# Reordering the head of a recurrent attention and feed-forward kernel: later zeroing, fewer idle products, one early gate/value piece, earlier states

## The chip, the cores and the metric

The kernel runs on one core of one Trainium2 chip. The metric is the device time of one execution in microseconds. Before the change the median of three runs is 625.0 us (624.94 to 625.14). The profiled execution took 625.15 us, and its trace spans 623.3 us. Every time inside the kernel is counted from the start of that span.

## The reference

Two blocks follow each other. The first is a recurrence over time for 4 batches, 8 heads, 768 steps and head size 48:

```python
for t in range(S):
    cur = einsum('bhd,bhe->bhde', u[None] * k_t, v_t)
    y[:, :, t] = einsum('bhd,bhde->bhe', r_t, state + cur)
    state = w[None, :, :, None] * state + einsum('bhd,bhe->bhde', k_t, v_t)
```

The second is a feed-forward block on the result, reshaped to 3072 tokens of 384 numbers: `(silu(x @ w_gate) * (x @ w_val)) @ w_out`, with 1536 inner columns. Everything is float32.

## The kernel before

The kernel cuts time into chunks of 128 steps. One chunk of one batch is a unit, so there are 24 units, and units 0 to 3 are the first chunks of the four batches. Inside a unit the recurrence becomes products of matrices: k and r are transposed and scaled by powers of the decay w (turn), their product gives a score matrix (scores) that is copied under a mask into At, whose diagonal holds the term of u (own_product, own_sum, diagonal). At times v gives the unit's outputs (outputs), and k times v adds to the batch's state Z (update). Unit 4 is the second chunk of batch 0 and so the first that reads a state.

The order in which the Python code emits the instructions is the order in which each engine runs them. There is no scheduler behind it. Engines wait for each other by semaphores.

The parts used below (cuts marked with ...):

```python
dve, pool, act, pe, sp = nc.vector, nc.gpsimd, nc.scalar, nc.tensor, nc.sync
ps_a = ... (name="ps_a", bufs=4, PSUM)      # scores, transposes, outputs, states
...
def own_product(i):                          # GpSimd, two instructions
    pool.tensor_mul(rk, rl, kl)
    pool.tensor_mul(rk, rk, ub[:])
def own_sum(i):                              # VectorE
    dve.tensor_reduce(dus[i][:], rks.pop(i), axis=AX.X, op=ALU.add)
def scale_k(i):
    pool.tensor_mul(khat[i % 4][:, :, 0:D], raw(i)[0], kscale[:])
def diagonal(i):                             # four heads on ScalarE, four on GpSimd
    small.extend(lambda h=h: act.activation(At[i % 2][:, h, :], ident[:], AF.Identity, scale=du[:, h : h + 1]) ...)
    pool.tensor_mul(At[i % 2][:, on_act:H], ident ..., du ...)
def turn(i):
    for tp, t, dst, table in zip(...):
        for a in range(HP):
            pe.transpose(tp[:, a, :], pair(t, a), ident[:])
        if i < 4:
            dve.tensor_mul(dst[:], tp[:], table)
        else:
            act.copy(dst[:], tp[:])
def scores(i):
    ...                                      # eight products into two PSUM tiles
    for e in range(2):
        dve.copy_predicated(At[i % 2] ..., mask ..., ps[e][:])
def outputs(i):
    ...                                      # products At x v, and from unit 4 on Z x rT
    act.copy(xT[:, i % NX, :, :], ps[:])
def update(i):
    ...                                      # products k x v into u_ps
    for e in range(2):
        if c == 0:
            dve.tensor_mul(ze, ps[rows], w)  # w is w128
        else:
            dve.tensor_add(ze, ps[rows], ze)
            pool.tensor_mul(ze, ze, w)
def gate_value(g, f):                        # a "piece": six products
    ...
    act.activation(sg[:], gv[:, 0, :], AF.Sigmoid)
    dve.tensor_mul(sg[:], sg[:], gv[:, 0, :])
    dve.tensor_mul(hT[g][:, f, :], sg[:], gv[:, 1, :])
```

The weights of the second block come in 18 chunks. Each is rounded on three engines before TensorE uses it: ScalarE makes a scaled high part (round_high) and a low part (round_low), VectorE puts the bits in place (round_dve), and GpSimd adds the low part (add_low for half a chunk, round_pool for a whole one). The low part has two buffers, so round_low of a chunk waits until GpSimd has added the low part of the chunk two before it.

`warm(n)` issues n products of the identity with itself whose results nobody reads. They keep TensorE busy while it would otherwise wait. `feed(1)` emits the next piece, once its weights are rounded.

The head of the program, in the order of emission:

```python
for z in Z:
    pool.memset(z[:], 0.0)
... # loads of w, of k and r of units 0 and 1, u, first weights, v
make_identity(nc, ident[:])                  # GpSimd
warm(18)
pool.memset(mask[:], 1.0) ...
... # decay tables on VectorE, pw and pv
own_product(0)
turn(0); natural_tables(); own_sum(0); diagonal(0)
own_product(1); load(2); load_weights(); load_v(2); warm(3)
turn(1); load(3); load_v(3); scores(0)
own_sum(1); diagonal(1)
... # first half of weight chunk 0
scores(1); warm(2); scale_k(0); add_low(0, 0); outputs(0)
... # first half of weight chunk 1
own_product(2); scale_k(1); outputs(1); queue(0)
for n in range(2):
    round_high(n, 1, n); round_dve(n, 1); add_low(n, 1)
load_weights()
turn(2); feed(1); own_sum(2); diagonal(2)
own_product(3); turn(3)
dve.tensor_copy(w128[:].unsqueeze(2), pw[:, :, 0:1])
scores(2); update(0); update(1)
own_sum(3); diagonal(3); scores(3)
scale_k(2); outputs(2); load(4)
round_act(); feed(1)
outputs(3); scale_k(3)
round_act(); round_pool(); scale(4); load_v(4); feed(1)
update(2); update(3)
round_pool(); own_product(4); load(5); feed(1)
...
```

From here a loop over the units follows, with pieces of the feed-forward block fed between their parts.

Of the kernel before, what the change touches and what calls it, by code (L numbers as in the profile page):

```python
# [22 lines left out]
def fast(  # L23
# [44 lines left out]
    dve, pool, act, pe, sp = nc.vector, nc.gpsimd, nc.scalar, nc.tensor, nc.sync  # L68
# [6 lines left out]
    w128 = cst.tile([P, HP], FP32, name="w128")  # L75
# [11 lines left out]
    Z = [cst.tile([P, HP, D2], FP32, name=f"Z{b}") for b in range(B)]  # L87
# [14 lines left out]
    def rhat_of(i):  # L102
        return rhat[i % 2 if i < BLOCKS else i % 4 // 2]

    def raw(i):

        if i < 4:
            return khat[i][:, :, 0:D], rhat[i % 2][:, :, 0:D]
        return k_ld[i % 2][:], r_ld[i % 2][:]
# [32 lines left out]
    def next_chunk(stage):  # L142
        n = done[stage]
        done[stage] = min(n + 1, NW)
        return n if n < NW else None

    def load_weights():
        n = next_chunk("load")
        if n is not None:
            src = chunks[n][0].bitcast(INT32)  # L150
            bits[n] = three.tile([P, WN, 2], INT32, name="w_bits", tag="w_bits")
            sp.dma_start(
                out=bits[n][:].rearrange("p (c f) two -> p c (f two)", c=src.shape[1]), in_=src
            )
# [13 lines left out]
    def round_high(n, half, bank):  # L168
        hi = halves(bits[n][:, :, 1], n)[half]
        ps, tag = ((ps_w, "w_mag"), (ps_o, "o"))[bank]  # L170
        mag = ps.tile([P, WN // 2], INT32, name="w_mag", tag=tag)
        mags[n, half] = mag[:].rearrange("p (c f) -> p c f", c=hi.shape[1])
        act.activation(
            mags[n, half].bitcast(FP32), hi.bitcast(FP32), AF.Copy, scale=float(2.0**-112)
        )

    def round_low(n):
        lows[n] = two.tile([P, WN], INT32, name="w_low", tag="w_low")
        act.activation(
            lows[n][:], bits[n][:, :, 0].bitcast(UINT32), AF.Copy, scale=float(2.0**-29)  # L180
        )

    def round_dve(n, half):
        hi = mags.pop((n, half))
        f = hi.shape[2]
        dst = chunks[n][1].bitcast(INT32)
        dst = dst[:, :, half * f : half * f + f] if hi.shape[1] == 3 else dst[:, half : half + 1]
        dve.tensor_scalar(dst, hi, -(1 << 31), None, ALU.bitwise_and)
        dve.scalar_tensor_tensor(dst, hi, 3, dst, ALU.logical_shift_left, ALU.bitwise_or)

    def add_low(n, half):

        dst = chunks[n][1].bitcast(INT32)
        f = dst.shape[2] // 2
        cols = slice(half * f, half * f + f)
        low = lows[n][:].rearrange("p (c f) -> p c f", c=dst.shape[1])
        pool.tensor_tensor(dst[:, :, cols], dst[:, :, cols], low[:, :, cols], ALU.add)

    def round_act(next_load=1):
        n = next_chunk("act")  # L200
        if n is not None:
            round_high(n, 0, 0)
            round_low(n)
            round_dve(n, 0)
            round_high(n, 1, 1)
            round_dve(n, 1)
            del bits[n]
            for _ in range(next_load):
                load_weights()
# [15 lines left out]
    def own_product(i):  # L225
        kl, rl = raw(i)
        rk = two.tile([P, H, D], FP32, name="rk", tag="rk")[:]
        pool.tensor_mul(rk, rl, kl)  # L228
        pool.tensor_mul(rk, rk, ub[:])
        rks[i] = rk  # L230

    def own_sum(i):
        dus[i] = three.tile([P, H], FP32, name="du", tag="du")
        dve.tensor_reduce(dus[i][:], rks.pop(i), axis=AX.X, op=ALU.add)
# [4 lines left out]
        dve.memset(t[:, :, D:64], 0.0)  # L239
    dve.memset(hats[:, 0:6, :, D:64], 0.0)  # L240
    dve.memset(wcol[:], 1.0)
    for z in Z:
        pool.memset(z[:], 0.0)
    for e in range(2):
        sp.dma_start(out=wcol[64 * e : 64 * e + D, :], in_=w.rearrange("(a e) d -> e d a", e=2)[e])
    load(0)
# [12 lines left out]
    def warm(n):  # L259

        ps = ps_a.tile([P, HP, P], FP32, name="warm", tag="a")
        for _ in range(n):
            pe.matmul(ps[:, 0, :], ident[:], ident[:], start=True, stop=True)

    warm(18)

    pool.memset(mask[:], 1.0)
    pool.affine_select(
        out=mask[:], in_=mask[:], compare_op=ALU.is_gt, fill=0.0,
        base=0, pattern=[[1, P]], channel_multiplier=-1,  # L270
    )
    dve.tensor_scalar(held[:], wcol[:], W_LOW, W_HIGH, ALU.max, ALU.min)
    tables = two.tile([P, 2, HP, P + 32], FP32, name="tables", tag="hT")
    pw, pv = tables[:, 0, :, 0 : P + 1], tables[:, 1, :, 0:P]
    dve.memset(pw[:, :, P : P + 1], 1.0)
    dve.tensor_copy(pw[:, :, P - 1 : P], held[:].unsqueeze(2))
    for l in range(7):
        n = 1 << l
# [19 lines left out]
    def scale_k(i):  # L298
        pool.tensor_mul(khat[i % 4][:, :, 0:D], raw(i)[0], kscale[:])  # L299
# [4 lines left out]
    def natural_tables():  # L304
        for t, dst in ((pw[:, :, 1 : P + 1], kscale), (pv, rscale)):
            t_ps = ps_a.tile([P, HP, P], FP32, name="t_ps", tag="a")
            for a in range(HP):
                pe.transpose(t_ps[:, a, :], t[:, a, :], ident[:])
            act.copy(dst[:], t_ps[:].rearrange("p a (e x) -> p (a e) x", e=2)[:, :, 0:D])
# [5 lines left out]
    def diagonal(i):  # L315

        du = dus.pop(i)
        on_act = HP if i < 4 else H
        small.extend(
            lambda h=h: act.activation(  # L320
                At[i % 2][:, h, :], ident[:], AF.Identity, scale=du[:, h : h + 1]
            )
            for h in range(on_act)
        )
        if on_act < H:
            n = H - on_act
            pool.tensor_mul(
                At[i % 2][:, on_act:H], ident[:].unsqueeze(1).to_broadcast([P, n, P]),
                du[:, on_act:H].unsqueeze(2).to_broadcast([P, n, P]),
            )  # L330

    def pair(t, a):
        return t[:, 2 * a : 2 * a + 2, :].rearrange("p e d -> p (e d)")

    def turn(i):
        kr = khat[i % 4], rhat_of(i)
        tps = [ps_a.tile([P, HP, P], FP32, name="tp", tag="a") for _ in kr]
        turned[i] = three.tile([P, HP, P], FP32, name="rT", tag="rT")
        for tp, t, dst, table in zip(tps, kr, (kT[i % 2], turned[i]), (pw[:, :, 1 : P + 1], pv)):
# [6 lines that stand above are left out]
# [69 lines left out]
    def update(i):  # L415
        c, b = divmod(i, B)
        if c == NCH - 1:
            return
        kh, vl, z = khat[i % 4], v_ld[i % 4], Z[b]
        ps = ps_a.tile([P, HP, D], FP32, name="u_ps", tag="a")  # L420
        for a in range(HP):
            for q in range(4):
                e, half = divmod(q, 2)
                pe.matmul(  # L424
                    ps[32 * q : 32 * q + 32, a, :], kh[:, 2 * a + e, 32 * half : 32 * half + 32],
                    vl[:, a, 64 * e : 64 * e + D],
                    start=True, stop=True, skip_group_check=True,
                )
        for e in range(2):
            rows = slice(64 * e, 64 * e + D)  # L430
            ze = z[rows, :, D * e : D * e + D]
            w = w128[rows].unsqueeze(2).to_broadcast([D, HP, D])
            if c == 0:
                dve.tensor_mul(ze, ps[rows], w)
# [3 lines that stand above are left out]
# [238 lines left out]
    def feed(n, pops=1):  # L676
        for _ in range(n):
            ready = [k for k, (need, _) in enumerate(todo) if need <= done["pool"] + len(summed)]
            if ready:
                todo.pop(ready[0])[1]()  # L680
            for _ in range(min(pops, len(small))):
                small.popleft()()
# [40 lines left out]
    def flush():  # L723
        while small:
            small.popleft()()
# [2 lines left out]
    turn(0)  # L728
    natural_tables()
    own_sum(0)  # L730
    diagonal(0)
    flush()
    own_product(1)
# [20 lines left out]
    round_low(1)  # L754
    round_dve(1, 0)
    add_low(1, 0)
    own_product(2)
    scale_k(1)
    outputs(1)
    queue(0)  # L760
    for n in range(2):
        round_high(n, 1, n)
        round_dve(n, 1)
        add_low(n, 1)
        del bits[n], lows[n]
    done.update(act=2, pool=2)
    load_weights()
    turn(2)
    feed(1)
    own_sum(2)  # L770
    diagonal(2)
    flush()
    own_product(3)
    turn(3)
    dve.tensor_copy(w128[:].unsqueeze(2), pw[:, :, 0:1])
    scores(2)
    update(0)
    update(1)
# [8 lines left out]
    feed(1)  # L787
    outputs(3)
    scale_k(3)
    round_act()  # L790
    round_pool()
    scale(4)
    load_v(4)
    feed(1)
    update(2)
    update(3)
    round_pool()
    own_product(4)
    load(5)
# [464 lines left out]
```

## Time and profile before

| what | value |
|---|---|
| time, median of three runs | 625.0 us |
| span of the trace | 623.3 us |
| TensorE busy | 611.0 us |
| TensorE busy from 600 us to the end (23.3 us) | 17.98 us |
| GpSimd busy from 41.0 to 54.7 us (13.7 us) | 13.46 us |
| VectorE busy from 20.7 to 30.0 us (9.3 us) | 9.04 us |
| zeroing of the four states, GpSimd | 0.80 to 2.28 us |
| first product of TensorE | 2.84 us |
| transposes of unit 3, second half | 25.34 us |
| outputs of unit 4, first product | 57.76 us |

PE is TensorE, PEld its weight loads, DVE VectorE, ACT ScalarE, POOL GpSimd, SP SyncE, which only issues transfers here. In the list of waits a line names who waited, for whom, the total in us, how often, and the longest. In the chain of waits a line has start, length, and what filled that time; the chain is followed back from the last instruction to whatever released it. In a timeline a line has start, length, engine, source line, operation, output and inputs, and shapes. L341 is turn, L379 and L384 are scores, L409 is outputs, L424 and L434 are update, L448 to L456 are a gate/value piece, L228 and L229 are own_product, L234 is own_sum, L299 is scale_k, L173, L179, L188, L189, L197 and L216 are the rounding of weights.

### The profile page before, as it was taken

The page shows a single profiled execution, that of the slowest core. Times are in us where ns is not written, and L with a number is a line of the kernel's source. Part 1 is how long each engine was busy: PE and PEld are TensorE (multiplying, and loading weights), DVE is VectorE, ACT ScalarE, POOL GpSimd, SP SyncE. Part 2 cuts the span into 40 slices and gives each one's busy share as a digit, 9 for nine tenths or more (in the row PEclk, how much of TensorE's full clock was granted, in tenths as well). Part 3 has the DMA queues.
Part 4 walks back from the last instruction along what each step waited for, and adds up shares of the span by engine and source line. Part 5 has one row for each costly group of instructions (what it writes and reads, how often), then busy time and mean ns, then how long its engine had stood idle before and what let it go on. Part 6 is the DMA issues. An engine that isn't in the chain of part 4 may idle for free.

```text
span 623.3 us, 13014 instructions
## 1 busy us (share of the span) xinstructions
PE 611.0 (98%) x5040; PEld 552.1 (89%) x5040; DVE 358.6 (58%) x751; ACT 238.9 (38%) x647; POOL 296.9 (48%) x350
## 2 busy tenths in 40 slices
PE   8799999999999999999999999999999999999996
PEld 7688888899888899888899888899988899988896
DVE  6888997373566574466575355574354463355460
ACT  3368785312444412344331335422243321233310
POOL 4789789935556315364452636341334211443110
PEclk9999999999999999999999999999999999999999
DMA  7989873233232213322223312221000000000001
GB/s 187 218 215 252 260 242 65 50 62 82 57 60 34 40 16 76 65 42 46 44 34 70 78 16 32 31 41 38 26 1 2 2 0 26 26 1 2 1 2 56
DMA packets 138008, 40.47 MB, mean 65 GB/s; under 512 B 128592, under 2 KB 131792, under 8 KB 137936
## 3 DMA queue, kind: packets, MB, share of 16 engines
q1 hardware_dynamic: 134480, 34.82, 26.4%
q10 hardware_dynamic: 3456, 4.72, 2.1%
q8 instruction: 42, 0.69, 0.5%
q14 instruction: 30, 0.25, 0.1%
HBM read 28.51 MB, written 4.72 MB: 53 GB/s over the span
## 4 chain that ended last, share of the span: by engine, by line
PE 90%; POOL 2%; DMA 1%; ACT 1%; DVE 1%; issue 0%; SPq 0%; ACTq 0%; POOLq 0%
PE c_b L625 25%; PE c_a L625 21%; PE o_f L519 13%; PE o_a L519 8%; PE gv L448 7%; PE o_b L519 6%; PE y_ps L409 5%; PE s_ps L379 3%; PE u_ps L424 1%; PE tp L341 1%; DMA r_ld<-in_r_dram 1%; POOL wg L216 1%; POOL wv L216 1%; POOL rk L228 0%; POOL hats L299 0%
## 5 line engine op out<-in xcount | busy, mean ns | idle before, releaser
L609 POOL TENSOR_TENSOR hT<-hT,u 128x256 f32<-128x256 f32 x60 | 47.0, 785 | 148.7 <-DVE hT L608 121.6
L632 ACT COPY u<-c_a 128x256 f32<-128x256 f32 x120 | 44.5, 371 | 85.8 <-PE c_a L625 83.3
L625 PE MATMUL c_a<-t,wv 128*128 128x256 f32 x240 | 72.1, 382 | 0.1
L625 PE MATMUL c_b<-xT,wg 128*128 128x256 f32 x240 | 71.7, 380 | 0.0
L605 ACT ACTIVATE sg<-hT 128x256 f32<-128x256 f32 x120 | 50.0, 416 | 52.5 <-DVE hT L634 33.8
L320 ACT ACTIVATE At<-ident,du 128x128 f32<-128x128 f32 x176 | 62.0, 398 | 16.0 <-DVE o_sb L533 7.2
L625 PE MATMUL c_b<-xT,s 128*128 128x256 f32 x240 | 61.7, 380 | 0.0
L639 DVE TENSOR_TENSOR u<-u,c_b 128x256 f32<-128x256 f32 x60 | 25.1, 419 | 60.5 <-PE c_b L625 55.4
L625 PEld LDWEIGHTS c_a<-t,wv 128*128 128x128 f32 x240 | 45.0, 190 | 6.8 <-ACT u L632 1.2
L625 PEld LDWEIGHTS c_b<-xT,s 128*128 128x128 f32 x240 | 45.3, 190 | 6.5
L625 PEld LDWEIGHTS c_b<-xT,wg 128*128 128x128 f32 x240 | 45.4, 190 | 5.9
L634 DVE TENSOR_TENSOR hT<-p,c_b 128x256 f32<-128x256 f32 x60 | 25.2, 420 | 41.7 <-PE c_b L625 39.1
L585 POOL TENSOR_TENSOR s<-wv,wg 128x256 f32<-128x256 f32 x24 | 17.6, 734 | 65.5 <-PE o_f L519 50.8
L384 DVE COPY_PREDICATED At<-mask,s_ps 128x512 f32<-128x512 int32 x48 | 33.0, 741 | 21.3 <-PE s_ps L379 12.4
L302 POOL TENSOR_TENSOR hats<-r_ld,rscale 128x384 f32<-128x384 f32 x20 | 20.8, 1040 | 35.3 <-DMA hats<-hats 25.2
L448 PE MATMUL gv<-xT,wg 128*128 128x256 f32 x144 | 36.7, 391 | 0.6 <-ACT xT L413 0.6
L637 DVE TENSOR_TENSOR hT<-hT,c_a 128x256 f32<-128x256 f32 x60 | 25.3, 421 | 19.5 <-PE c_a L625 18.3
L641 DVE TENSOR_TENSOR hT<-u,c_b 128x256 f32<-128x256 f32 x60 | 25.2, 421 | 19.4 <-PE c_b L625 19.2
L625 PE MATMUL c_b<-t,s 128*128 128x256 f32 x120 | 36.2, 383 | 0.0
L409 PE MATMUL y_ps<-At,v_ld 128*32 128x128 f32 x768 | 34.9, 273 | 1.3 <-DVE At L384 1.3
L625 PE MATMUL c_b<-xT,wv 128*128 128x256 f32 x120 | 35.9, 381 | 0.0
L625 PE MATMUL c_a<-t,s 128*128 128x256 f32 x120 | 35.8, 380 | 0.0
(135 smaller groups left out, 1384.3 us busy)
## 6 DMA issues: line engine op xcount, KB each, us to landing
hats<-hats SPq DMA_DIRECT2D x192, 32.0 KB, 2.0
w_bits<-in_moe_w_gate_dram SPq DMA_DIRECT2D x6, 768.0 KB, 6.4
v_ld<-in_v_dram SPq DMA_DIRECT2D x48, 96.0 KB, 3.3
w_bits<-in_moe_w_val_dram SPq DMA_DIRECT2D x6, 768.0 KB, 6.3
w_bits<-in_moe_w_out_dram SPq DMA_DIRECT2D x6, 768.0 KB, 6.7
out_dram<-o_sb ACTq DMA_DIRECT2D x24, 192.0 KB, 1.9
k_ld<-in_k_dram SPq DMA_DIRECT2D x20, 192.0 KB, 3.1
r_ld<-in_r_dram SPq DMA_DIRECT2D x20, 192.0 KB, 3.8
```

Source lines behind the costliest of these rows:

```text
L320: lambda h=h: act.activation(At[i % 2][:, h, :], ident[:], AF.Identity, scale=du[:, h : h + 1])
L384: dve.copy_predicated(At[i % 2][:].rearrange("p (a e) t -> p a e t", e=2)[:, :, e], mask[:].bitcast(INT32).unsqueeze(1).to_broadcast([P, H ...
L409: pe.matmul(ps[32 * q : 32 * q + 32, cc, :], *x, start=start, stop=stop, skip_group_check=True,)
L448: pe.matmul(gv[:, o, :].rearrange("p (i t) -> p i t", i=2), wt[:, c, P * f : P * (f + 1)], xT[:, 2 * g % NX : 2 * g % NX + 2, c, :], start ...
L519: pe.matmul(ps, lhs[:, f, :], rhs[:, f, :], start=(f == 0 and n in (0, 1, 4)), stop=(f == FH - 1), skip_group_check=True,)
L605: act.activation(x[what, f][:], h[j], AF.Sigmoid)
L609: pool.tensor_mul(h[1], h[1], x.pop(("u3", f))[:])
L625: pe.matmul(ps.rearrange("p (i t) -> p i t", i=2), lhs, rhs, start=first, stop=what not in ("p2", "p5", "p4", "p3"), skip_group_check=True,)
L632: act.copy(x[nm, f][:], ps)
L634: dve.tensor_add(h[0], x.pop(("p1", f))[:], ps)
L637: dve.tensor_mul(h[0], h[0], ps)
L641: dve.tensor_add(h[1], x.pop(("u2", f))[:], ps)
```

## The change

It changes the order of emission and takes five idle products away; nothing that the result depends on is left out. The states are zeroed after the identity and the mask, so that TensorE can begin earlier. There are 13 idle products ahead of the first transposes instead of 18. The last row of the decay table is copied to w128 early. The scaling of k of unit 1 goes ahead of rk of unit 2. The first gate/value piece goes ahead of turning unit 2, and the second halves of the first two weight chunks get their low parts after unit 2's diagonal. The states of units 2 and 3 go ahead of the third piece, to fill the wait for the outputs of unit 3.

```diff
@@ setup
-    for z in Z:
-        pool.memset(z[:], 0.0)
@@
-    warm(18)
+    warm(13)
     pool.memset(mask[:], 1.0)
     pool.affine_select(...)
+    for z in Z:
+        pool.memset(z[:], 0.0)
@@
     own_sum(0)
+    dve.tensor_copy(w128[:].unsqueeze(2), pw[:, :, 0:1])
     diagonal(0)
@@
+    scale_k(1)
     own_product(2)
-    scale_k(1)
     outputs(1)
     queue(0)
     for n in range(2):
         round_high(n, 1, n)
         round_dve(n, 1)
+    load_weights()
+    feed(1)
+    turn(2)
+    own_sum(2)
+    diagonal(2)
+    for n in range(2):
         add_low(n, 1)
         del bits[n], lows[n]
     done.update(act=2, pool=2)
-    load_weights()
-    turn(2)
-    feed(1)
-    own_sum(2)
-    diagonal(2)
     flush()
     own_product(3)
     turn(3)
-    dve.tensor_copy(w128[:].unsqueeze(2), pw[:, :, 0:1])
     scores(2)
@@
     outputs(3)
     scale_k(3)
+    update(2)
+    update(3)
     round_act()
     round_pool()
     scale(4)
     load_v(4)
     feed(1)
-    update(2)
-    update(3)
     round_pool()
     own_product(4)
```

## The prediction, made before the changed kernel ran

> **What bounds the kernel now.** I read the page's busy times first, then busy time by stretch, then the waits of TensorE, then the chain that ended last.
>
> ```profile
> PE 611.0 (98%) x5040; PEld 552.1 (89%) x5040; DVE 358.6 (58%) x751; ACT 238.9 (38%) x647; POOL 296.9 (48%) x350
> ```
>
> ```profile
> 20.70:30.00 9.30, 7.67 (x123) 6.07 (x123) 9.04 (x18) 1.95 (x6) 7.77 (x8) 1.00 0.99 212
> ...
> 40.00:50.00 10.00, 10.00 (x66) 8.79 (x65) 7.64 (x18) 8.06 (x20) 9.84 (x10) 1.00 0.94 204
> 50.00:58.00 8.00, 7.71 (x57) 6.42 (x59) 6.97 (x15) 6.03 (x14) 7.92 (x7) 1.00 1.00 278
> ...
> 62.00:100.00 38.00, 38.00 (x453) 33.02 (x453) 35.13 (x75) 30.71 (x74) 31.34 (x29) 1.00 0.76 223
> 100.00:300.00 200.00, 200.00 (x1814) 181.27 (x1813) 110.95 (x232) 72.50 (x211) 110.58 (x132) 1.00 0.29 53
> ```
>
> The columns after the length of the stretch are busy time of PE, PEld, DVE, ACT, POOL, then clock, DMA share and GB/s. From 58 us to 600 us TensorE never waits, so the program's end is fixed by the moment at which that dense run starts. The change touches only what stands ahead of it. What ends last ahead of it is told by two views:
>
> ```profile
> PE warm L263 <- POOL ident masks.py:199: 2.8, 1, 2.8
> PE y_ps L409 <- DVE At L384: 1.3, 2, 1.2
> PE tp L341 <- DMA hats<-in_k_dram: 0.8, 1, 0.8
> PE gv L448 <- ACT xT L413: 0.6, 1, 0.6
> PE tp L341 <- DMA hats<-in_r_dram: 0.5, 2, 0.3
> PE s_ps L379 <- DVE At L384: 0.4, 1, 0.4
> PE y_ps L409 <- ACT kT L345: 0.3, 1, 0.3
> ```
>
> ```profile
> 52.90 1.80 POOL wv L216
> 54.70 0.02 issue
> 54.73 0.93 ACT w_low L179
> ...
> 57.24 0.48 ACT kT L345
> 57.72 0.04 issue
> 57.76 1.75 PE y_ps L409 x56
> ```
>
> The last wait of TensorE (0.3 us) ends at 57.76 us, in the outputs of unit 4, and ScalarE ended it, itself released by a GpSimd addition. GpSimd is busy 9.84 of 10.00 us and 7.92 of 8.00 us there. So **GpSimd's dense run from about 39 us sets the end**, with only 0.3 us of TensorE's own work behind it. Time that TensorE gains earlier is not kept unless GpSimd's run starts earlier too. Where that run starts:
>
> ```profile
> 37.78 0.56 DVE L189 SCALAR_TENSOR_TENSOR wv<-w_mag,wv 128x384 int32<-128x384 int32 x1
> ...
> 39.30 1.82 POOL L216 TENSOR_TENSOR wv<-wv,w_low 128x768 int32<-128x768 int32 x1
> ...
> 39.54 1.47 DVE L434 TENSOR_TENSOR Z<-u_ps,w 48x192 f32<-48x192 f32 x4
> ```
>
> VectorE has rounded this piece of wv at 38.34, GpSimd takes it at 39.30. The slack is about 0.8 us, and the 1.47 us of state updates stand behind it, not ahead.
>
> **What the Trainium skill says.**
> - "SBUF — State Buffer", section "Who interferes with whom": a VectorE copy in a two-port mode and a GpSimd instruction exclude each other, and whichever issues first keeps the ports for the whole instruction. The trace agrees: the four-column copy of the table took 0.17 us at 4.74, with GpSimd idle, and 0.96 us at 26.61 as w128, while GpSimd's rk product ran from 26.54 to 27.55.
> - "TensorE: Matmul & The Clock Gate", section "What's actually happening": TensorE runs at half clock until it has been busy for about 3.4 us, by free-running windows. Here the first 22 of the 36 records of idle products take 4.86 us (2.84 to 7.70 us), 0.22 us each, and the last 14 take 1.97 us, 0.14 each. That is about 5 us of slow running, longer than one such window; the measurement decides.
> - "DMA: Bandwidth & Descriptors", section "Specifications": transfers under 512 B do not reach line rate. Of the 33,013 packets of the first 62 us, 29,037 are under 512 B, and DMA is busy at a share of 0.99 from 20.7 to 30. No run here separates packet size from load.
>
> **Part 1: the zeroing and the idle products.** GpSimd zeroes the states for 1.48 us ahead of the identity. Afterwards the identity is ready 1.42 us earlier (its memset starts at 0.80 instead of 2.22), near 1.4 us. The zeroing falls where GpSimd waits 4.2 us for r, and costs nothing. Each idle product has two records (36 for 18), so 13 have 26. At 0.22 us a record, nearly all slow, they take 5.7 us and end at 7.1 to 7.3 instead of 9.67. r of unit 0 lands at 3.50 + 3.9 = 7.4, so the transposes can start there. VectorE is held by the decay tables until 7.63 + 1.43 = 9.06, so its first product starts at 9.1 instead of 10.14: **1.1 us earlier**.
>
> How far does it carry? The outputs of unit 1 need its v, issued at about 11.2 and landing 6.5 us later, at 17.7. Unit 1's masked scores should be ready at 17.4 instead of 18.46, so those outputs run from 17.7 to 18.8 (before: ending 19.59), and xT of unit 1 is there at 19.35 instead of 20.12: 0.8 us. Then r of unit 3 lands at 19.56 + 5.6 = 25.2, and these transfers are not earlier, since the DMA queue issues them back to back. So turning unit 3 stays at 25.3 to 26.0. The gain of the head becomes a TensorE wait of some 2 us ahead of 25.3.
>
> **Part 2: the gate/value piece ahead of turning unit 2.** It runs from 19.4 to 22.15 instead of 20.80 to 23.56, without the transposes to fill the wait for xT. VectorE now does its two products (0.42 us each) ahead of the scaling of unit 2. It ends the rounding at about 22.1, waits for the sigmoid until 22.6, then products to 23.4, kT and rT to 24.65, and du of unit 2 from 24.6 to 25.15 instead of 24.81 to 25.36: **0.2 us earlier**.
>
> **Part 3: the w128 copy.** Moved to where GpSimd waits for du of unit 0, it should cost 0.17 us. Its 0.96 us at 26.61 is gone. Unit 2's masked copies can start when the scores are there, at 27.1 instead of 27.49. That is 0.4 us on VectorE, but see part 4.
>
> **Part 4: the two late additions.** They pass from ahead of unit 2's diagonal to behind it. GpSimd: diagonal from 25.3, 1.04; additions 2 x 1.00; rk of unit 3, two of 1.0. It ends at about 30.35 instead of 28.62. du of unit 3, which ran at 30.22, can start at 30.4: **0.2 us later**, and it releases the diagonal and masked scores of unit 3 and then the rounding of wg. The 0.4 us of part 3 are lost in this new wait.
>
> **Part 5: states of units 2 and 3 ahead of the third piece.** On TensorE the 0.89 us of u_ps fill the 0.6 us wait for xT. On VectorE four updates (1.46 us, about 1.4 with overlap) come ahead of the rounding of wv. That was ready at 38.34; now at 38.34 + 0.2 + 1.4 = 39.9, and the addition can start at about 40.05 (0.15 us after VectorE, as for wg at 35.44 and 35.59), instead of 39.30. **0.7 us later**, with a dense run behind it.
>
> **Sum.** TensorE gains 0.6 us and perhaps 0.4 us more ahead of 38 us, and waits that much longer at unit 4's outputs. These come 0.7 us later, less up to 0.2 us of bubbles in GpSimd's run (13.46 busy of 13.70 from 41 to 54.7). So 625.0 + 0.5 to 0.7. I take 625.4, because two terms of 0.2 us could each turn.
>
> **Rivals.**
> - *TensorE's saved time counts.* If GpSimd's run were not tight, the wait of 0.6 us, the 0.3 us and part of the 2.8 us would come off: 623.5 to 624.5. For it: TensorE is 98% busy. Against: its waits after 26 us are 1.3 us in all, and GpSimd's run ends later than TensorE now.
> - *du of unit 2 comes much earlier.* Were it ready at 24.5 or before, rk of unit 3 would be done with VectorE's state updates, the 0.4 us of part 3 would be kept, and the wv addition would be only 0.2 us late: 625.0 to 625.2. Against: the v landing at 17.7 and the rounding on VectorE.
> - *The copy loses the ports to GpSimd's diagonal of unit 0*, released by the same du. Then it costs about 1 us near 11 us; most of that is hidden ahead of the 25.2 us landing: 625.5 to 626.
> - *Transfers move.* They fill the queue; an earlier release could bring r of unit 3 sooner. Each us there could be worth up to 0.5: 624.5.
>
> **Range and chances.** The steps are tenths of a microsecond on a base repeating within 0.2 us. The rivals span 623.5 to 626. I take 624.2 to 626.2. 2% is 12.5 us, over the whole TensorE idle time of 12.3 us, so "within 2%" has 0.988, and faster and slower by more have 0.006 each.
>
> **What would show it.** Right: first product on TensorE near 1.4 us; r of unit 3 at 25.2; du of unit 3 at 30.3 or later behind GpSimd's rk; wv addition near 40; a TensorE wait of over 1 us ahead of unit 4's outputs, then a dense run of the same length. Wrong: the wv addition at 39.3 or before, or unit 4's outputs ahead of 57.7; then the Rivals hold.

## The result, and the profile after

The changed kernel takes 627.9 us (median of six runs, 627.1 to 628.8), beside 625.1 us of the kernel before on the same chip. The ratio is 1.0045, with a 95% interval of 1.0032 to 1.0058. The prediction was 625.4 us with a range of 624.2 to 626.2. Its direction was right, its size was not. The profiled execution has a span of 625.7 us, against 623.3.

The page of the changed kernel, busy times and the granted clock of TensorE in 40 slices:

```profile
PE 611.3 (98%) x5030; PEld 551.0 (88%) x5030; DVE 358.3 (57%) x751; ACT 239.3 (38%) x647; POOL 297.3 (48%) x350
...
PEclk9899999999999999999999999999999999999999
```

The busy times are those of before within about 1 us, so no work was added. But the second slice of the clock (15.6 to 31 us) shows an 8. Busy time by stretch (length, then PE, PEld, DVE, ACT, POOL, clock, DMA share, GB/s):

```profile
20.70:30.00 9.30, 6.83 (x107) 5.73 (x108) 6.31 (x12) 1.67 (x5) 6.28 (x7) 0.82 1.08 209
...
40.00:50.00 10.00, 8.93 (x59) 7.36 (x58) 7.35 (x16) 6.49 (x15) 9.20 (x9) 1.00 0.82 192
50.00:58.00 8.00, 8.00 (x53) 6.96 (x52) 6.24 (x14) 5.96 (x15) 7.92 (x7) 1.00 0.97 238
```

Three things differ from before. From 20.7 to 30 us TensorE is busy 6.83 us instead of 7.67 although its clock is lower (0.82 instead of 1.00). From 40 to 50 us it waits for 1.1 us where it was dense. GpSimd is still dense from 41 us on, so the same engine sets the end. The waits of TensorE in the changed kernel (who, for whom, total, how often, longest):

```profile
PE tp L341 <- DMA hats<-in_k_dram: 2.3, 1, 2.3
PE warm L261 <- POOL ident masks.py:199: 1.4, 1, 1.4
PE y_ps L409 <- DVE At L384: 1.2, 1, 1.2
...
PE y_ps L409 <- ACT kT L345: 0.8, 1, 0.8
```

The wait for the identity fell from 2.8 to 1.4 us, as intended, and the wait for k of unit 3 grew from 0.8 to 2.3 us. The timeline of the changed kernel shows what follows (start, length, engine, line, operation, tiles; the wait ahead in brackets):

```profile
24.71 0.66 PE L341 MATMUL tp<-ident,hats 128*128 128x128 f32 x4 [2.28 <-DMA hats<-in_k_dram]
...
26.11 1.88 PE L379 MATMUL s_ps<-rT,kT 48*128 48x128 f32 x16
...
28.12 1.37 DVE L384 COPY_PREDICATED At<-mask,s_ps 128x512 f32<-128x512 int32 x2 [1.21 <-PE s_ps L379]
28.70 1.00 POOL L229 TENSOR_TENSOR rk<-rk,ub 128x384 f32<-128x384 f32 x1
...
30.87 0.55 DVE L234 TENSOR_REDUCE du<-rk 128x8 f32<-128x384 f32 x1
...
36.62 1.84 POOL L216 TENSOR_TENSOR wg<-wg,w_low 128x768 int32<-128x768 int32 x1 [2.07 <-ACT w_mag L173]
37.17 1.46 DVE L434 TENSOR_TENSOR Z<-u_ps,w 48x192 f32<-48x192 f32 x4
...
41.01 1.84 POOL L216 TENSOR_TENSOR wv<-wv,w_low 128x768 int32<-128x768 int32 x1 [0.64 <-DVE wv L189]
```

The same steps in the kernel before:

```profile
25.89 1.16 PE L379 MATMUL s_ps<-rT,kT 48*128 48x128 f32 x16
...
30.22 0.55 DVE L234 TENSOR_REDUCE du<-rk 128x8 f32<-128x384 f32 x1
...
35.59 1.83 POOL L216 TENSOR_TENSOR wg<-wg,w_low 128x768 int32<-128x768 int32 x1 [1.68 <-DVE wg L189]
```

After the 2.28 us wait the scores of unit 2 take 1.88 us; before, the same 16 records took 1.16. The clock record of the trace (when the granted clock changed, and to what) has the reason: half clock from 26.37 us for 3.41 us. In the kernel before there is no fall ahead of 600 us. Everything on VectorE behind those scores is late: du of unit 3 by 0.65 us, the wg addition on GpSimd by 1.03 (36.62 against 35.59). The wv addition is later by 1.71 (41.01 against 39.30) and now waits 0.64 us for VectorE, with the state updates ahead of it. The chain of waits of the changed kernel (start, length, what filled it) is the chain of before, 1.75 us later:

```profile
54.65 1.80 POOL wv L216
...
56.48 0.93 ACT w_low L179
...
58.98 0.48 ACT kT L345
59.46 0.04 issue
59.51 1.75 PE y_ps L409 x56
```

From unit 4's outputs to the end the profile has 566.2 us, before 565.6.

### The profile page after: what moved, and what is told of

Same layout as the page of the kernel before. It is cut to its first block, busy times and chain, and to the rows that moved or that the text cites. A ratio compares the mean times of both kernels' runs of the same rounds, so it can differ in the third digit from the quotient of the medians.

```text
span 625.7 us, 12991 instructions
## 1 busy us (share of the span) xinstructions
PE 611.3 (98%) x5030; PEld 551.0 (88%) x5030; DVE 358.3 (57%) x751; ACT 239.3 (38%) x647; POOL 297.3 (48%) x350
## 4 chain that ended last, share of the span: by engine, by line
PE 86%; POOL 3%; DVE 2%; SPq 2%; ACT 1%; DMA 1%; issue 0%; ACTq 0%; POOLq 0%; DVEq 0%
PE c_b L625 23%; PE c_a L625 19%; PE o_f L519 13%; PE o_a L519 8%; PE gv L448 7%; PE o_b L519 6%; PE y_ps L409 5%; PE s_ps L379 3%; SPq L356 2%; PE u_ps L424 1%; PE tp L341 1%; DMA r_ld<-in_r_dram 1%; POOL wv L216 1%; POOL rk L228 0%; ACT At L320 0%
## 5 line engine op out<-in xcount | busy, mean ns | idle before, releaser
L634 DVE TENSOR_TENSOR hT<-p,c_b 128x256 f32<-128x256 f32 x60 | 25.2, 420 | 41.9 <-PE c_b L625 39.3
L641 DVE TENSOR_TENSOR hT<-u,c_b 128x256 f32<-128x256 f32 x60 | 25.2, 421 | 19.7 <-PE c_b L625 19.6
L637 DVE TENSOR_TENSOR hT<-hT,c_a 128x256 f32<-128x256 f32 x60 | 25.3, 422 | 19.0 <-PE c_a L625 17.4
L625 PE MATMUL c_a<-xT,wg 128*128 128x256 f32 x120 | 35.8, 380 | 0.0
```

What stands on the lines that cost most here:

```text
L625: pe.matmul(ps.rearrange("p (i t) -> p i t", i=2), lhs, rhs, start=first, stop=what not in ("p2", "p5", "p4", "p3"), skip_group_check=True,)
L634: dve.tensor_add(h[0], x.pop(("p1", f))[:], ps)
L637: dve.tensor_mul(h[0], h[0], ps)
L641: dve.tensor_add(h[1], x.pop(("u2", f))[:], ps)
```

## The experiments

The theories. **A**: the longer waits of TensorE let its clock fall, and slow products delay VectorE and then GpSimd. **B**, the prediction's own: the order on VectorE and GpSimd alone costs it, above all the states ahead of the wv rounding. **C** came up on the way: the place of an instruction in VectorE's stream. Each kernel was compared with the kernel before on its own chip; on these later chips that one took 626.0 to 626.3 us, and in its trace there (before_again) most of the early transfers landed 0.6 to 0.9 us later than in the first profile.

One table carries most readings. "Least busy" is the lowest share of any stretch of 3.41 us ending between 10 and 30 us in which TensorE executed products, worked out from its records. "Fall" is start and length of half clock ahead of 60 us. "Copy late" is from the end of GpSimd's diagonal of unit 3 to the masked copy that it releases. The next two count from the wg addition: to the wv addition, and to unit 4's outputs. All but the ratio are from the one profiled execution.

| kernel | ratio to before, interval | least busy | fall (us) | copy late | wg to wv | wg to unit 4 |
|---|---|---|---|---|---|---|
| before | | 0.61 | none | 0.04 | 3.71 | 22.17 |
| before_again | | 0.44 | none | 0.03 | 3.71 | 22.16 |
| after | 1.0045, 1.0032 to 1.0058 | 0.28 | 26.37, 3.41 | 0.39 | 4.39 | 22.89 |
| after_again | 1.0038, 1.0021 to 1.0054 | 0.36 | 19.72, 3.41 | 0.40 | 4.39 | 22.88 |
| fill8 | 1.0034, 1.0023 to 1.0046 | 0.43 | none | 0.39 | 4.39 | 22.91 |
| states_back | 1.0032, 1.0020 to 1.0043 | 0.38 | 18.96, 6.83 | 0.39 | 3.70 | 22.18 |
| fill8_states_back | 1.0035, 1.0024 to 1.0045 | 0.41 | 18.22, 6.83 | 0.39 | 3.71 | 22.17 |
| warm18 | 1.0032, 1.0020 to 1.0045 | 0.38 | 19.29, 3.41 | 0.39 | 4.39 | 22.85 |
| head_only | 1.0009, 0.9999 to 1.0019 | 0.42 | none | 0.03 | 3.71 | 22.17 |
| order_only | 1.0023, 1.0015 to 1.0032 | 0.38 | 28.09, 3.41 | 0.39 | 4.40 | 22.84 |
| fill3 | 1.0012, 1.0005 to 1.0020 | 0.72 | none | 0.39 | 4.40 | 22.87 |
| fill3_again | 1.0011, 1.0000 to 1.0022 | 0.73 | none | 0.40 | 4.40 | 22.86 |
| fill3_pad | 1.0006, 0.9995 to 1.0016 | 0.70 | none | 0.03 | 4.39 | 22.86 |
| states_only | 1.0013, 1.0006 to 1.0019 | 0.44 | none | 0.03 | 4.40 | 22.90 |
| w128_early | 0.9999, 0.9987 to 1.0010 | 0.46 | none | 0.40 | 3.72 | 22.24 |
| fill3_states_back | 1.0005, 0.9997 to 1.0013 | 0.71 | none | 0.40 | 3.74 | 22.23 |
| fill3_scale4 | 1.0001, 0.9993 to 1.0009 | 0.67 | none | 0.40 | 2.90 | 21.75 |
| fill3_scale4_pad | 0.9994, 0.9986 to 1.0001 | 0.74 | none | 0.03 | 2.70 | 21.67 |
| scale4_before | 0.9999, 0.9989 to 1.0008 | 0.56 | none | 0.03 | 2.68 | 22.13 |
| scale4_again | 0.9988, 0.9979 to 0.9998 | 0.17 | 19.53, 3.41 | 0.03 | 2.68 | 21.86 |

### First group: fill one wait, undo one part

fill8 fills the 2.3 us wait of the profile with idle products; states_back undoes Part 5; the third does both; warm18 gives the head its 18 idle products back.

```diff
 fill8 (against the changed kernel)
     turn(2)
+    warm(8)
     own_sum(2)
 states_back
-    update(2)
-    update(3)
     round_act()
     round_pool()
     scale(4)
     load_v(4)
     feed(1)
+    update(2)
+    update(3)
 warm18
-    warm(13)
+    warm(18)
```

> The changed kernel, with eight idle products (16 records at 0.14 us, 2.2 us) between the transposes of unit 2 and those of unit 3, where TensorE waited 2.3 us for k of unit 3 before its clock fell to half for 3.4 us from 26.37 us. Theory A (the wait lets the clock fall, and the slow scores and states push the whole chain back): the clock stays at full speed ahead of 60 us, the scores of unit 2 take 1.16 us again instead of 1.88, the masked copies of unit 2 start near 27.3 us instead of 28.12, du of unit 3 near 30.0 instead of 30.87, and the outputs of unit 4 near 58.6 instead of 59.51; the time falls by about 0.9 us, to 627.0. Rival B (the new order on GpSimd and VectorE alone makes the loss, as the prediction had it): no change, 627.9, and outputs of unit 4 at 59.5.

> The changed kernel with the states of units 2 and 3 put back behind the third piece. Rival B: VectorE rounds wv 1.4 us earlier, near 39.5 us, the addition on GpSimd follows the scaling of unit 4 without a wait, near 40.4 instead of 41.01, and the outputs of unit 4 come near 58.9 instead of 59.51: 627.3. The clock still falls ahead of the scores of unit 2. Theory A, if it were the whole of the loss: no change, 627.9.

> Both edits: eight idle products ahead of turning unit 3, and the states of units 2 and 3 behind the third piece. If A and B each make a part of the loss and add up: the wv addition near 39.5, the outputs of unit 4 near 58.0, 625.3. If only one of them counts: the same as the better of the two alone.

> The changed kernel with 18 idle products at the head again. They end near 8.3 us, and VectorE is held by the decay tables until 8.9 anyway, so the transposes of unit 0 lose at most 0.2 us. If the number of idle products is a cause of its own: 1 us less. A and B both say: it is not, the wait for unit 3 and the fall of the clock stay, 627.7 to 628.1.

Measured: 628.3, 628.5, 628.4 and 628.0 us, against 626.1 of the kernel before. None of the four came back, so by time alone theory A had missed with fill8. The profiles say more. In the three that fell it was not at 26 us but at 18 to 19 us, ahead of the first gate/value piece and behind a wait that fill8 does not fill (outputs of unit 1, 1.7 to 2.0 us for v). In states_back the piece then took 5.5 us; in the changed kernel it had taken 2.8. fill8's profiled execution had no fall, yet its times spread from 626.4 to 630.4. One filled wait isn't enough if another can trip the clock. The number of idle products at the head is not the cause.

### Second group: the parts of the change, and all waits filled

head_only is the kernel before with the later zeroing and 13 idle products. order_only is the changed kernel with the old head. fill3 fills three waits of the changed kernel.

```diff
 head_only (against the kernel before)
-    for z in Z: pool.memset(z[:], 0.0)      # first of all
-    warm(18)
+    warm(13)
     pool.memset(mask[:], 1.0) ...
+    for z in Z: pool.memset(z[:], 0.0)
 order_only (against the changed kernel): the same lines the other way round
 fill3 (against the changed kernel)
     own_product(2)
+    warm(5)
     outputs(1)
     ...
     load_weights()
+    warm(2)
     feed(1)
     turn(2)
+    warm(8)
     own_sum(2)
```

> The kernel before, with the head of the change alone: states zeroed after the mask, and 13 idle products instead of 18; nothing else is moved. Theory A (an earlier head only makes TensorE wait for transfers that are not earlier, and the waits let its clock fall to half for 3.4 or 6.8 us just where units 2 and 3 are turned): the clock falls between 18 and 30 us in the profile or in many of the runs, the times spread more widely than the kernel before, and the median is 1 to 2 us above it. Rival B (the moved instructions make the loss): the outputs of unit 4 stay within 0.2 us of the kernel before on the same chip, and so does the time. Rival C (the head helps, as the change intended): 0.5 to 1 us faster.

> The changed kernel with the head of the kernel before: states zeroed first, 18 idle products. All the moved instructions stay moved. Theory A: no fall of the clock, a narrow spread; what is left is the order on GpSimd and VectorE, 0 to 0.7 us above the kernel before. Rival B: the whole loss stays, 2.2 us or more.

> The changed kernel with idle products in all three waits of TensorE between 15 and 25 us: five ahead of the outputs of unit 1, two ahead of the first piece, eight ahead of turning unit 3 (15 x 0.27 us, 4.1 us in all). Theory A: the clock never falls ahead of 60 us, the times spread no more than those of the kernel before, and the time is 0.3 to 1.0 us above it. Rival B: the loss stays at 2 us or more with the clock at full speed. A third way: the idle products themselves come too late on a chip where the transfers land early, and then they cost up to 1 us.

> The kernel before, unchanged, profiled on the chip of these runs, so that landings and stages can be compared on one chip. If the landings of v of unit 1 and r of unit 3 differ by about 1 us from the first profile (17.7 and 25.2 us), the outputs of unit 4 move with them; the clock stays at full speed ahead of 60 us.

Measured: 626.5, 627.6 and 626.9 us against 626.2. head_only gains nothing, though its first product runs 1.4 us earlier. Theory A had asked for a loss of 1 to 2 us here, and by the medians that missed (0.2 us). In order_only the clock fell at 28.09 us, which had not been expected: the moved order alone opens waits that are long enough. fill3 shows no fall ahead of 60 us, and its 14 runs lie between 626.7 and 627.5, far closer than the others.

### Is it the clock? Both on one chip

after_again and fill3_again repeat two kernels unchanged, side by side.

> The changed kernel once more, beside the others of this group on one chip. Theory A (TensorE's waits ahead of 26 us let the granted clock fall to half, which delays scores and pieces): clock at 0.5 for 3.4 or 6.8 us somewhere between 18 and 30 us, time 1.5 to 2.8 us over the kernel before, and 0.7 us or more over fill3_again. Rival (the fall costs nothing, all of the loss is the order on VectorE and GpSimd): time within 0.3 us of fill3_again.

> fill3 once more on the chip of after_again. Theory A: no fall of the clock ahead of 60 us, 0.7 to 1.0 us over the kernel before. First masked copy of unit 3 starts 0.39 us behind the diagonal that releases it, as in the earlier run.

Measured: 629.0 and 626.8 us, before 626.0. The difference is 2.2 us, and the intervals of the two ratios only just touch (1.0021 and 1.0022). Busy time by stretch of after_again and then of fill3_again, same columns as above:

```profile
14.99:18.40 3.41, 1.24 (x35) 0.76 (x26) 3.00 (x7) 2.90 (x8) 2.97 (x3) 1.00 1.26 256
18.40:25.00 6.60, 5.94 (x47) 4.94 (x48) 2.75 (x6) 1.86 (x5) 3.97 (x4) 0.74 1.04 224
```

```profile
14.99:18.40 3.41, 2.95 (x48) 2.35 (x51) 3.10 (x7) 3.21 (x8) 2.98 (x3) 1.00 1.30 247
18.40:25.00 6.60, 6.58 (x66) 5.86 (x62) 4.24 (x9) 1.79 (x5) 3.98 (x4) 1.00 1.09 230
```

The same for the profile on record, after and then fill3, where the wait fell later:

```profile
22.19:25.60 3.41, 0.94 (x8) 0.50 (x7) 2.52 (x6) 0.95 (x4) 0.91 (x1) 1.00 0.94 124
25.60:30.00 4.40, 4.40 (x91) 3.89 (x93) 3.06 (x6) 0.33 (x2) 4.02 (x5) 0.61 1.08 274
```

```profile
22.19:25.60 3.41, 3.38 (x30) 3.07 (x28) 2.50 (x5) 0.45 (x2) 1.13 (x3) 1.00 0.85 139
25.60:30.00 4.40, 3.81 (x98) 3.03 (x98) 3.34 (x7) 1.22 (x4) 4.32 (x5) 1.00 1.06 277
```

In each pair the first line shows the cause, the second the effect: a stretch of 3.41 us with TensorE busy for 0.94 or 1.24 us is followed by a clock of 0.61 or 0.74; filled to 3.38 or 2.95 us it is followed by 1.00. The table makes it sharper. Seven of the 20 executions fell, and they are the seven whose emptiest stretch was at most 0.41 busy; from 0.42 up none did. The edge is not that sharp: 0.410 (fill8_states_back) and 0.415 (head_only) stand on either side of it. In each trace the clock changes only on a grid of 3.41 us. Counted on this grid, the last window ahead of a fall was 0.28 to 0.43 busy in six of the seven and 0.57 in order_only, while windows of 0.46 and 0.48 (head_only, fill8) had no fall. So near the edge it also matters where the wait lies on the grid, and order_only is not explained by this count.

The table has one execution of each kernel; the mean clock of every run is on record. A fall of 3.41 us takes about 0.003 off it, and the half clock at the end of the span up to 0.0025. In the 82 runs of the six rows with the idle products of fill3 it was never under 0.997. In the 107 runs of the seven rows with the moved order and without those idle products (after to warm18, and order_only) it was 0.996 or less 67 times; their median is 628.7 us, that of the other 40 runs 627.3. fill8 was that low in 12 of 20 runs (629.0 against 627.5 us) and head_only in 11 of 22 (627.0 against 626.1), which goes with their wide spread. The kernel before was that low in 29 of 232 runs on these chips. So A holds, and B as the whole story falls.

### What is left: the states, alone and taken back

states_only is the kernel before with Part 5 alone. fill3_states_back is fill3 with Part 5 undone, by the edit of states_back.

```diff
 states_only (against the kernel before)
     scale_k(3)
+    update(2)
+    update(3)
     round_act()
     round_pool()
     scale(4)
     load_v(4)
     feed(1)
-    update(2)
-    update(3)
```

> The kernel before with one part of the change alone: the states of units 2 and 3 go ahead of the third piece; idle products, zeroing, the first piece and the late additions stay as they were. TensorE's waits ahead of 31 us are then those of before, so no fall of the granted clock is expected there. The prediction's Part 5: the wv addition on GpSimd comes 0.7 us later (it stood 0.8 us behind its input, and four updates of 1.4 us come ahead of that input), unit 4's outputs 0.7 us later, time 0.6 to 0.8 us over the kernel before. The rival (all that is lost beyond the clock comes from the earlier first piece and the masked copies of unit 3 that start 0.39 us late): no difference over 0.2 us here.

> The changed kernel with the idle products of fill3 (TensorE's waits filled) and the states of units 2 and 3 back behind the third piece. Clock full ahead of 60 us. Part 5 of the prediction: the wv addition comes 0.6 to 0.7 us earlier than in fill3 (about 40.2 instead of 40.88), unit 4's outputs about 58.7 instead of 59.34, time 0 to 0.2 us over the kernel before. The rival (the remainder is not the states): time as fill3, about 0.7 us over before.

Measured: 627.0 and 626.5 us against 626.1. The timeline of states_only, then of before_again, at the two additions:

```profile
36.52 1.83 POOL L216 TENSOR_TENSOR wg<-wg,w_low 128x768 int32<-128x768 int32 x1 [1.69 <-DVE wg L189]
37.08 1.45 DVE L434 TENSOR_TENSOR Z<-u_ps,w 48x192 f32<-48x192 f32 x4
...
40.92 1.85 POOL L216 TENSOR_TENSOR wv<-wv,w_low 128x768 int32<-128x768 int32 x1 [0.64 <-DVE wv L189]
```

```profile
36.06 1.83 POOL L216 TENSOR_TENSOR wg<-wg,w_low 128x768 int32<-128x768 int32 x1 [1.68 <-DVE wg L189]
...
39.77 1.82 POOL L216 TENSOR_TENSOR wv<-wv,w_low 128x768 int32<-128x768 int32 x1
```

With the state updates between the two additions GpSimd waits 0.64 us for the rounding of wv. From wg to wv it takes 4.40 instead of 3.71 us, and from wg to unit 4's outputs 22.90 instead of 22.16. The table shows these two values in every kernel without the later edit to scale(4), whatever the clock did: near 22.9 with the states ahead, near 22.2 with them behind. Part 5 costs 0.7 us.

### A masked copy that starts 0.39 us late

The "copy late" column splits the kernels in another way. In the built programs the masked copy of unit 3 is VectorE's instruction number 65, counted from 0, in the old order, and number 64 in the changed one, because the early copy to w128 needs one semaphore instruction less. Two kernels test the number alone: fill3_pad repeats the copy to w128, so that all later numbers rise by one; w128_early moves only that copy in the kernel before, so that they fall by one.

```diff
 fill3_pad (against fill3)
     dve.tensor_copy(w128[:].unsqueeze(2), pw[:, :, 0:1])
+    dve.tensor_copy(w128[:].unsqueeze(2), pw[:, :, 0:1])
 w128_early (against the kernel before)
     own_sum(0)
+    dve.tensor_copy(w128[:].unsqueeze(2), pw[:, :, 0:1])
     ...
     turn(3)
-    dve.tensor_copy(w128[:].unsqueeze(2), pw[:, :, 0:1])
```

> fill3 with the copy to w128 written twice, one after the other, near 11 us where VectorE waits. The result is the same; every later VectorE instruction has a number one higher. If the place in the instruction stream makes the masked copy of unit 3 start late, it starts 0.03 us behind the diagonal and not 0.39, the wg addition comes 0.35 us earlier, the outputs of unit 4 too, and the time is 0.3 to 0.4 us under fill3_again. Rival (the delay belongs to the moved order itself: data, ports, semaphores): the delay stays at 0.39 and the time is as fill3_again.

> The kernel before with only the copy to w128 moved behind the sum of unit 0. It takes one semaphore instruction less, so the masked copy of unit 3 has number 64 as in the changed kernel, though nothing else of the order has moved. If the place in the stream is the cause, it starts 0.39 us behind the diagonal, unit 4's outputs are 0.3 to 0.4 us later, and the time 0.2 to 0.4 us over the kernel before. Rival: 0.03 us as before and no difference in time, or a little less by the copy that GpSimd held up.

The timelines of fill3_again (number 64), fill3_pad (65) and w128_early (64):

```profile
31.73 1.04 POOL L327 TENSOR_TENSOR At<-ident,du 128x512 f32<-128x512 f32 x1 [0.75 <-DVE du L234]
33.16 1.37 DVE L384 COPY_PREDICATED At<-mask,s_ps 128x512 f32<-128x512 int32 x2 [1.58 <-POOL At L327]
```

```profile
32.29 1.04 POOL L327 TENSOR_TENSOR At<-ident,du 128x512 f32<-128x512 f32 x1 [0.90 <-DVE du L234]
33.36 1.38 DVE L384 COPY_PREDICATED At<-mask,s_ps 128x512 f32<-128x512 int32 x2 [1.22 <-POOL At L327]
```

```profile
31.81 1.04 POOL L327 TENSOR_TENSOR At<-ident,du 128x512 f32<-128x512 f32 x1 [2.33 <-DVE du L234]
33.25 1.37 DVE L384 COPY_PREDICATED At<-mask,s_ps 128x512 f32<-128x512 int32 x2 [1.58 <-POOL At L327]
```

The diagonal ends at 32.77, 33.33 and 32.85; the copy starts 0.40, 0.03 and 0.40 us later. The number decides, in both directions, and the other 17 traced executions agree: C holds. The times (626.5 against 626.8 of fill3_again; 626.1 against 626.0 of before) don't resolve 0.4 us, since transfers landed differently by as much. Why number 64 waits is not shown. Two facts of the traces bear on it. Just ahead of the copy stands a semaphore instruction that waits for the diagonals until 32.7 us in fill3_again; in the old order number 64 is that semaphore instruction itself, reached some 2 us earlier. And one 8 KB packet that the trace calls "instruction" starts 0.7 to 1.0 us behind the copy in the 12 executions where it is number 64, and 2.3 to 2.8 us ahead of it in the 8 where it is 65. The trace doesn't say for which engine.

### Can the gap be used?

GpSimd waits 1.7 us ahead of the wg addition. Scaling unit 4 (two products of 1.0 us) fits in there.

```diff
 scale4_before (against the kernel before), scale4_again the same
     round_act()
+    scale(4)
     round_pool()
-    scale(4)
     load_v(4)
```

fill3_scale4 is fill3_states_back with this edit, fill3_scale4_pad adds the repeated copy to w128.

> As fill3_states_back, and the scaling of unit 4 on GpSimd goes ahead of the wg addition, where GpSimd waits 1.7 us for the rounding of wg. If GpSimd's dense run from the wv addition sets the end, as the prediction has it, that scaling (two products of 0.5 to 0.8 us) leaves the dense run: unit 4's outputs about 0.7 us earlier than in fill3_states_back, and the time 0.2 to 0.7 us under the kernel before. If GpSimd's run doesn't set the end, no difference from fill3_states_back.

> The kernel before with only the scaling of unit 4 moved ahead of the wg addition. GpSimd's dense run ends about 0.8 us earlier; TensorE waited only 0.3 us for it at unit 4's outputs and 1.3 us in all after 26 us, so 0.3 us are gained at unit 4 and the time is 0.2 to 0.4 us under the kernel before. If GpSimd's run doesn't set the end: no difference.

> The changed order with all three causes taken out: TensorE's waits filled with idle products, the states of units 2 and 3 behind the third piece, the copy to w128 written twice[...]; and the scaling of unit 4 moved into GpSimd's wait ahead of the wg addition. If these are the whole loss: masked copy of unit 3 0.03 us behind the diagonal, outputs of unit 4 21.8 us after the wg addition as in fill3_scale4 (before: 22.2), and the time 0.2 to 0.5 us under the kernel before. If something of the loss is not found yet: at the time of before or over it.

> The kernel before with the scaling of unit 4 ahead of the wg addition, once more, since the first run (0.4 us less by the medians) had an interval of 0.9989 to 1.0008. If GpSimd's run sets the end and TensorE has 0.3 to 0.5 us of wait behind it at the outputs of unit 4: 0.3 to 0.4 us under the kernel before. If not: no difference.

Measured: 626.2 and 625.7 us against 626.1; then 626.1 and 625.8 against 626.3. The timeline of fill3_scale4_pad:

```profile
34.60 1.02 POOL L299 TENSOR_TENSOR hats<-k_ld,kscale 128x384 f32<-128x384 f32 x1
...
35.58 1.01 POOL L302 TENSOR_TENSOR hats<-r_ld,rscale 128x384 f32<-128x384 f32 x1
...
36.53 1.83 POOL L216 TENSOR_TENSOR wg<-wg,w_low 128x768 int32<-128x768 int32 x1
...
39.23 1.83 POOL L216 TENSOR_TENSOR wv<-wv,w_low 128x768 int32<-128x768 int32 x1 [0.86 <-DVE wv L189]
...
58.20 0.42 PE L409 MATMUL y_ps<-rT,Z 112*32 112x128 f32 x8
```

The wv addition comes 2.70 us after wg instead of 3.71, and the wait of TensorE at unit 4's products is gone. Of the 1.0 us that GpSimd gains little reaches unit 4, though: counted from wg its outputs come after 21.67 us instead of 22.17, and in scale4_before after 22.13. The chain of waits has moved. In scale4_before it goes through a weight transfer that lands at 54.72 us and ScalarE's work behind it, in fill3_scale4_pad through TensorE's own products. So GpSimd's run sets the end only by a few tenths of a microsecond. With all three causes out and the gap used, the changed order is level with before (0.9994, interval 0.9986 to 1.0001). The old order with the gap used is faster in its second measurement (0.9988, interval 0.9979 to 0.9998) and unclear in its first (0.9999, interval 0.9989 to 1.0008): 0.4 and 0.5 us by the two pairs of medians. That it beats the kernel before is thus shown by one measurement of two, and by little; none of it needs the change. In the second measurement the profiled execution had a fall at 19.53 us, after the emptiest stretch of all (0.17), so the old order can trip the clock too. The second half of v of unit 1 landed there at 18.85 us, in scale4_before at 17.55.

## Why the prediction was wrong in size

- **The bound: right.** GpSimd's run from the wv addition set unit 4's outputs before and after, and TensorE was dense from there but for one wait of 0.36 us (below).
- **Part 1: numbers right, conclusion wrong. This is the step that failed.** The first product came at 1.43 us, the idle products ended at 6.71 (0.20 us a record, not 0.22), and r of unit 3 landed at 25.4 (predicted 25.2). VectorE's first product came at 8.85 us (predicted 9.1). By the clock record the slow running at the head lasted 5.4 us before and 4.5 us in the changed kernel (predicted about 5; 3.0 to 6.0 over the 20 executions). And the wait of "some 2 us ahead of 25.3" was there, 2.28 us. The prediction took this wait as free because TensorE doesn't bound there. It left TensorE busy for 0.94 us in 3.41, and half clock followed. The Trainium skill, "TensorE: Matmul & The Clock Gate", section "What's actually happening", has the array go back to half clock after at least one idle window of about 3.4 us. The lengths of the falls agree with such windows (3.41 and 6.83 us), but no window ahead of a fall was idle: the longest wait ahead of one was 2.3 us, and 0.41 of busy time in fill8_states_back did not prevent one. The prediction quoted this section for the head and did not apply it to the wait it had itself worked out. No rival named it either.
- **Part 2: right in kind, too cautious.** The piece ran from 18.73 to 21.56 (predicted 19.4 to 22.15), and du of unit 2 came at 24.00 instead of 24.6. The prediction had read the landing of v wrongly: it put it at 17.7 from an issue at 11.2, but in the profile of before the second half of v of unit 1 was issued at 10.65 and landed at 17.11; in the changed kernel it landed at 16.86.
- **Part 3: the copy right, its gain not seen.** The copy took 0.15 us at 10.50, with GpSimd idle (predicted 0.17), in agreement with the section on shared ports that the prediction cited. Masked copies of unit 2 started at 28.12, not 27.1: the scores took 0.72 us longer at half clock. Moving the copy also shifted the instruction numbers, a term of 0.36 us that the prediction couldn't have: nothing in the profile of before shows it.
- **Part 4: wrong.** rk of unit 3 was done at 29.70, not 30.35, because Part 2 came earlier, and VectorE, late by the clock, reached du of unit 3 only at 30.87. With the clock full, du of unit 3 moved by less than 0.1 us (30.75 in fill3, 30.68 in before_again). The two additions cost nothing there.
- **Part 5: right.** Predicted 0.7 us, measured 0.68 on GpSimd (4.39 less 3.71) and 0.72 at unit 4.
- **The sum.** Unit 4's outputs came 1.75 us later in the profile: 0.72 for the states and 1.03 ahead of the wg addition, of which 0.36 is the place in the stream (0.396 less 0.035) and 0.67 is left for the clock. In after_again the wg addition was 1.58 us later than in fill3_again, and the time 2.2 us longer. The prediction's 0.5 to 0.7 was the states alone.
- **Not settled:** the 0.6 us that the profile lost behind the start of unit 4's outputs. Of it 0.36 us is one wait of TensorE at 303.3 us, for ScalarE's copy p, which before doesn't have. In the other kernels this part took 565.6 to 566.4 us, and more in two, with no pattern that the edits explain; it was not tested. The range was too narrow because it allowed only for terms already on the list.

## What to carry to other kernels

An idle engine is not always free: before you open a wait on TensorE, find the emptiest 3.4 us stretch around it, and fill it with idle products if it comes near the 0.4 busy at which the clock fell here. Read the clock column stage by stage, since in the mean over the span a fall is a matter of the third decimal (0.996 here). Where an engine runs dense to the end, count what you put between its inputs and its first instruction; and where it has a gap just ahead, move work into the gap and look at what binds next: here 1.0 us on GpSimd gave 0.5 us or less.

## What the runs showed of the hardware that was not expected

- Ahead of 60 us, half clock came for 3.41 us, or twice that, 0.3 to 1.3 us after the end of a 3.41 us stretch with TensorE 0.17 to 0.41 busy; with 0.42 and over it didn't come, in 20 traced executions. In the two long falls TensorE was 0.81 busy in the first 3.41 us at half clock, in the five short ones 0.84 or more.
- The masked copy of unit 3 on VectorE started 0.39 to 0.40 us after its last release where it had number 64 in the stream (12 executions), and 0.03 to 0.04 us after it with number 65 (8 executions), whatever else had been changed.
- Transfers issued earlier did not land earlier: k and r of unit 3 were issued 1.3 to 1.4 us sooner in the changed kernel (17.54 and 18.23 us) and landed at 24.7 and 25.4, against 24.3 and 25.2 before.
